# A second level of seven-product multiplication for two of the seven products of Q, gate and up, with column sets chained across pairs

## The chip, the cores and the metric

The kernel runs on one core of one Trainium2 chip. The metric is the device time of one execution in microseconds (us). TensorE is written PE below, its weight loads PEld, VectorE DVE, ScalarE ACT, and SP is the engine that issues the DMAs. Every run reported here is fast, and the granted TensorE clock is 0.998 to 1.000 of full speed in all of them.

A ratio is the mean time of one kernel's fast runs over the mean of the other's fast runs of the same rounds, so it is not quite the ratio of the medians that are quoted beside it. The kernel before takes 747.55 us (median of 4 runs, 746.85 to 748.61).

## The reference

A layer norm feeds two branches. Branch A is linear attention with 32 heads over 2048 tokens, width 1024; branch B is a gated feed-forward layer of width 3584.

```python
xn  = layernorm(x)                                   # 2048 x 1024
q, k, v = split(xn @ wqkv)                           # 1024 x 3072
pq, pk  = phi(q), phi(k)                             # phi(t) = (t > 0 ? t + 1 : exp(t)) + 1e-6
s   = ((pq @ (pk^T v)) / (pq . sum(pk) + 1e-6)) @ wo # per head
b   = (silu(xn @ w_gate) * (xn @ w_up)) @ w_down     # 1024 x 3584, 3584 x 1024
out = x + s * silu(b)
```

## The kernel before

The kernel records every operation with the regions it reads and writes, orders each engine's operations by a list scheduler (earliest deadline first; PE may depart from program order by a window of six groups), and emits fixed instruction streams with semaphore waits. Nearly all operations therefore have one source line, that of a helper: read the groups by what they write and read. `ps` is PSUM (eight banks of 128x512 fp32), `W` holds weights and their sums, `X` and `P` hold the transposed `xn` of the first and second 1024 tokens (the two passes), `H` is the big result area, `TM` holds temporaries.

Already here each matrix product is a block product with seven instead of eight multiplications. One *set* is 256 weight columns against 1024 tokens: the weights are cut into 2 x 2 blocks (halves of K, halves of the columns), so are the tokens, and the seven block products are accumulated in PSUM banks. A product is 4 matmuls (K of 512 in steps of 128) of 512 columns. The sums of weight blocks that products 3, 5, 6 and 7 need are made by DVE when the weights have landed.

```python
def step(self, m):                        # one of the seven products of a set
    if m == 1:
        self.a = balloc(True);  self.grp(1, self.a, True)
        self.b = balloc()
        act(... ps[self.b], ps[self.a], ACT.Identity)        # bank b starts as a copy of P1
    elif m == 5:
        e = balloc(True);       self.grp(5, e, True)
        self.s5 = s5_ring.take();  act(... self.s5, ps[e], ACT.Identity);  bfree(e)
    elif m == 2:                          # P1 + P2 is result (0,0)
        self.grp(2, self.a, False);  self.out(0, 0, self.a)
    elif m == 6:
        self.grp(6, self.b, False);  self.c = balloc()
        tt(... ps[self.c], ps[self.b], self.s5, ALU.add)
    elif m == 7:
        self.grp(7, self.b, False);  d = self.dring.take()
        tt(... d, ps[self.b], self.s5, ALU.add);  self.evac(1, 1, d, ...)
    elif m == 3:  self.grp(3, self.c, False);  self.out(0, 1, self.c)
    elif m == 4:  self.grp(4, self.b, False);  self.out(1, 0, self.b)

# two sets run interleaved as a pair: (set, product)
PAIRSEQ = ((0,1),(0,5),(1,1),(0,2),(1,5),(0,6),(1,2),(1,6),(0,7),(0,3),(1,7),(0,4),(1,3),(1,4))

# --- cut ---
def gu_pair(p, n, stat, at=()):           # a pair is one gate set and one up set
    def ev_g(i, j, ap, r, bank):          # gate: ACT, Silu, PSUM to SBUF
        act(... s.ap(FP16), ap, ACT.Silu)
    def ev_u(i, j, ap, r, bank):          # up: DVE multiplies straight from PSUM into H
        tt(... o, ap, s.ap(FP16), ALU.mult)

order = [("q", 0), ("g", 0), ("q", 1)] + [("g", n) for n in range(1, 14)]   # per pass of 1024 tokens
```

After these 16 pairs a pass has the down products (the D stage, with the attention's last product beside it). The normalisation of the attention (ACT scales a broadcast reciprocal, DVE multiplies) runs beside gate/up pairs 2 and 3.

## Time and profile before

| | before |
|---|---|
| time, median | 747.55 us |
| span of the profiled run | 745.6 us |
| PE busy | 734.1 us (98%), 3522 matmuls |
| DVE busy | 541.1 us (73%) |
| ACT busy | 321.2 us (43%) |

These lines are the first part and the chain of the page: busy time, its share of the span, and the number of instructions; then the chain of work that ended last, by engine.

```profile
span 745.6 us, 9302 instructions
...
PE 734.1 (98%) x3522; PEld 330.4 (44%) x3522; DVE 541.1 (73%) x1010; ACT 321.2 (43%) x532; POOL 16.2 (2%) x35
...
PE 93%; DVE 2%; ACT 2%; DMA 2%; issue 0%; POOL 0%; SPq 0%
...
```

PE is busy almost throughout, and matmuls make 93% of the chain. A busy PE proves little by itself, because the end of a matmul is modelled (379 ns for one of 512 columns, while the next begins after 216). What does prove it is the distance of starts. In the steady gate/up stretch, 56 matmuls take 12.087 us, which is 56 x 215.8 ns. I call *hole* whatever lies between the starts of two neighbouring matmuls beyond what the first takes at its width. The small `Zh` matmuls (the attention's denominators, on 32 columns of the array) are an exception: PE loses about 0.1 us around each group of them with no other engine to wait for, and this is counted with the stream of matmuls, not as holes. Beyond the first 31 us the holes add up to 5.0 us, and 2.2 us of these are the last product's, at the end.

Busy time of each engine by stretches; the first number of a line is the stretch, the second its length. The stretches are Q and the first gate/up sets, the normalisation, steady gate/up with the D stage, the turn of the pass with Q of pass 2, and the normalisation of pass 2.

```profile
...
core 0: us, PE busy (x) PEld busy (x) DVE busy (x) ACT busy (x) POOL busy (x), PEclk, DMA share, GB/s
125.00:200.00 75.00, 74.24 (x358) 31.49 (x356) 55.28 (x109) 40.89 (x72) 0.00 (x0) 1.00 0.48 137
200.00:230.00 30.00, 29.85 (x139) 13.31 (x139) 28.32 (x54) 21.28 (x38) 0.00 (x0) 1.00 0.74 214
230.00:420.00 190.00, 190.00 (x882) 86.00 (x881) 131.56 (x218) 60.66 (x104) 0.00 (x0) 1.00 0.49 124
420.00:480.00 60.00, 59.57 (x286) 24.89 (x285) 44.62 (x86) 31.06 (x47) 0.00 (x0) 1.00 0.38 101
480.00:530.00 50.00, 50.00 (x234) 22.62 (x233) 43.16 (x77) 28.44 (x50) 0.00 (x0) 1.00 0.64 178
...
```

Only the first two and the fourth stretch have any PE idle at all. DVE is the second engine: 131.56 of 190 us in the long stretch.

Groups of instructions (line, engine, operation, written<-read, shapes, number | busy us, mean ns | idle before and what ended it):

```profile
...
L209 PE MATMUL ps<-X,W 128*128 128x512 f16 x1504 | 347.9, 379 | 1.8 <-DVE ps L344 1.2 <-DMA W<-m_scratch 0.5 <-DVE TM L344 0.2
...
L344 DVE TENSOR_TENSOR H<-ps,TM 128x512 f16<-128x512 f32 x84 | 57.3, 689 | 10.8 <-PE ps L209 10.7
...
L337 ACT ACT_TABLE_LOAD x10 | 12.8, 1283 | 1.0 <-PEq L1249 0.8
...
```

The second is up's eviction by DVE. The third: ten loads of an activation table, 1283 ns each, 12.8 us of ACT. They come where Exp (in phi of K and Q) and Silu (gate, D stage) alternate.

### The profile page before, as it was taken

To read this page: it belongs to the slowest core of one execution; us is meant where nothing else is said; L and a number is where in the kernel's file an instruction comes from. 1 tells how busy PE (TensorE), PEld (TensorE's weight loads), DVE (VectorE), ACT (ScalarE), POOL (GpSimd) and SP (SyncE) were. 2 spreads that over 40 slices of the span, in tenths; PEclk is the share of its full clock that TensorE was granted. 3 is DMA by queue.
4 is the path that set the end of the run, shared out by engine and by line. 5 is a ranking of instruction groups with operands and counts; after the bars stand their busy time and mean duration, and the time that the engine had idled before them with its cause. 6 is when DMAs were issued, how large, how long until landed. Compare 5 with 4: busy or idle time off the path is not lost.

```text
span 745.6 us, 9302 instructions
## 1 busy us (share of the span) xinstructions
PE 734.1 (98%) x3522; PEld 330.4 (44%) x3522; DVE 541.1 (73%) x1010; ACT 321.2 (43%) x532; POOL 16.2 (2%) x35
## 2 busy tenths in 40 slices
PE   7999999999999999999999999999999999999997
PEld 3444444434444444444444444344444444444442
DVE  6999757768797776876467677879876768557353
ACT  3677545565574343422232265547533433223131
POOL 2211100000000000000000000000000000000000
PEclk9999999999999999999999999999999999999999
DMA  9353125434682424371846733428627352274822
GB/s 302 94 113 86 29 56 176 108 103 129 191 234 81 113 57 113 100 227 41 199 114 154 181 88 84 114 81 229 203 61 222 104 150 68 68 150 109 193 65 49
DMA packets 168492, 93.92 MB, mean 126 GB/s; under 512 B 33024, under 2 KB 164352, under 8 KB 168448
## 3 DMA queue, kind: packets, MB, share of 16 engines
q1 hardware_dynamic: 168448, 93.34, 47.2%
q8 instruction: 27, 0.44, 0.3%
q14 instruction: 17, 0.14, 0.1%
HBM read 75.50 MB, written 10.62 MB: 115 GB/s over the span
## 4 chain that ended last, share of the span: by engine, by line
PE 93%; DVE 2%; ACT 2%; DMA 2%; issue 0%; POOL 0%; SPq 0%
PE ps L209 93%; DMA W<-m_scratch 1%; ACT H L337 1%; ACT TM L337 1%; DMA W<-in_A_x_dram 0%; DMA H<-r_scratch 0%; DVE TM L344 0%; DVE H L344 0%; ACT L337 0%; PE ps L216 0%; ACT X L337 0%; DVE stats L555 0%; DVE W L344 0%; DVE ps L344 0%; DVE TM L625 0%
## 5 line engine op out<-in xcount | busy, mean ns | idle before, releaser
L209 PE MATMUL ps<-X,W 128*128 128x512 f16 x1504 | 347.9, 379 | 1.8 <-DVE ps L344 1.2
L337 ACT ACTIVATE TM<-ps 128x512 f32<-128x512 f32 (+1 forms) x275 | 162.4, 597 | 252.5 <-PE ps L209 241.5
L209 PEld LDWEIGHTS ps<-X,W 128*128 128x128 f16 (+1 forms) x1504 | 144.6, 98 | 177.6 <-DVE ps L344 3.7
L209 PE MATMUL ps<-H,W 128*128 128x512 f16 (+1 forms) x896 | 205.3, 379 | 0.7 <-DVE TM L625 0.4
L344 DVE TENSOR_TENSOR W<-W 128x1024 f16<-128x1024 bf16 (+3 forms) x224 | 134.2, 628 | 15.4 <-DMA W<-in_B_w_down_dram 6.3
L209 PEld LDWEIGHTS ps<-H,W 128*128 128x128 f16 (+1 forms) x896 | 87.0, 98 | 105.6 <-DVE TM L625 0.9
L209 PE MATMUL ps<-P,W 128*128 128x512 f16 x512 | 123.0, 379 | 0.0
L344 DVE TENSOR_TENSOR ps<-ps,TM 128x512 f32<-128x512 f32 x94 | 65.5, 697 | 71.8 <-PE ps L209 71.7
L337 ACT ACTIVATE ps<-ps 128x512 f32<-128x512 f32 x94 | 55.0, 585 | 98.1 <-PE ps L209 96.1
L344 DVE TENSOR_TENSOR TM<-ps,TM 128x512 f32<-128x512 f32 x88 | 60.2, 684 | 46.3 <-PE ps L209 45.9
L209 PEld LDWEIGHTS ps<-P,W 128*128 128x128 f16 (+1 forms) x512 | 49.3, 98 | 59.3 <-issue 0.2
L344 DVE TENSOR_TENSOR H<-ps,TM 128x512 f16<-128x512 f32 (+1 forms) x91 | 62.1, 688 | 12.1 <-PE ps L209 11.8
L337 ACT ACTIVATE TM<-TM 128x512 f16<-128x512 f32 (+1 forms) x61 | 37.5, 616 | 40.1 <-DVE TM L344 34.9
L344 DVE TENSOR_TENSOR H<-H 128x1024 f16<-128x1024 f16 (+2 forms) x82 | 51.2, 633 | 3.6 <-ACT H L337 2.7
L344 DVE TENSOR_TENSOR TM<-TM 128x512 f16<-128x512 f16 (+1 forms) x63 | 26.0, 421 | 21.5 <-DMA TM<-TM 13.9
L209 PE MATMUL ps<-H,X 128*128 128x512 bf16 (+1 forms) x136 | 32.3, 379 | 1.0 <-ACT X L337 0.7
L624 DVE TENSOR_SCALAR TM<-TM 128x512 f16<-128x512 f16 x64 | 17.7, 288 | 17.3 <-ACT TM L337 16.9
L337 ACT ACTIVATE H<-ps 128x512 bf16<-128x512 f32 (+2 forms) x42 | 24.3, 613 | 11.3 <-PE ps L209 10.9
L344 DVE TENSOR_TENSOR W<-H 128x1024 f16<-128x1024 f16 x38 | 25.7, 686 | 3.7 <-PE ps L209 3.3
L337 ACT ACTIVATE H<-H,zc 128x512 bf16<-128x512 bf16 x32 | 21.6, 715 | 8.6 <-DMA H<-r_scratch 8.6
L209 PE MATMUL ps<-H,P 128*128 128x512 bf16 (+1 forms) x96 | 23.5, 379 | 0.0
L209 PE MATMUL ps<-W 128*128 128x512 f16 x76 | 22.1, 379 | 0.0
(69 smaller groups left out, 287.8 us busy)
## 6 DMA issues: line engine op xcount, KB each, us to landing
W<-in_B_w_gate_dram SPq DMA_DIRECT2D x28, 512.0 KB, 4.1
W<-in_B_w_up_dram SPq DMA_DIRECT2D x28, 512.0 KB, 5.3
W<-in_B_w_down_dram SPq DMA_DIRECT2D x16, 896.0 KB, 6.6
W<-in_A_x_dram SPq DMA_DIRECT2D x16, 256.0 KB, 3.4
H<-in_A_wqkv_dram SPq DMA_DIRECT2D x8, 512.0 KB, 8.1
W<-in_A_wqkv_dram SPq DMA_DIRECT2D x8, 512.0 KB, 5.2
H<-r_scratch SPq DMA_DIRECT2D x32, 128.0 KB, 3.6
q_scratch<-H SPq DMA_DIRECT2D x8, 512.0 KB, 3.9
```

The costliest lines, as they stand in the source:

```text
L209: last = h.matmul(o, l, r, start=st, stop=sp, skip_group_check=True)
L337: return PL.op("act", reads, writes, lambda h: h.activation(o, i, func, **kw), nel(o) / 1200.0 + (0.055 if src == "ps" else 0.095))
L344: return dve(reads, writes, lambda h: h.tensor_tensor(o, a, b, op), nel(o), 1.92 if fast else 0.96)
L624: dve([e.r], [b.r], lambda h: h.tensor_scalar(ba, ea, 1.0, EPS_PHI, ALU.min, ALU.add), 512, 2.6)
```

## The change

The intent is to take columns out of PE's stream. For products 1 and 5, two *neighbouring* sets multiply different weights with the same moving block. Together they are one product of 512 x 256 weights with 512 x 512 tokens, and that is again done in seven instead of eight inner products: K in two halves of 256, columns by set, tokens in two halves of 256. An inner product is two matmuls of 256 columns.

To have neighbouring sets side by side, a pair is now two gate sets or two up sets (512 weight columns, one DMA of 1 MB instead of two of 512 KB). The inner products form a chain of four parts (matmul, ACT copies, matmul, DVE sum, matmul, DVE sum, matmul), so the head of each pair is interleaved with the tail of the pair before, also from the last D set of pass 1 into Q of pass 2. Up is evicted by ACT into H and then multiplied by DVE in 16 bit, and its product 7 goes straight into H. Buffers were moved to make room. The first Q pair of pass 1 has no inner products.

```diff
+        QJ = (((), (1, 5)), ((1, 5), (1, 5)))
+        class Joint:                      # the seven inner products of product 1 or 5 of two sets
+            def step(self, part):
+                if part == 0:
+                    self.x, self.y = balloc(), balloc(True)
+                    self.grp(1, y, 0, True);  self.grp(5, y, 1)          # half banks
+                    act(... ps[x][:, 0:256], ps[y][:, 0:256], ACT.Identity)
+                    self.s = q_ring.take()
+                    act(... self.s, ps[y][:, 256:512], ACT.Identity)
+                elif part == 1:
+                    self.grp(6, y, 0);  self.grp(2, x, 0)
+                    tt(... ps[x][:, 256:512], ps[y][:, 0:256], s, ALU.add)
+                elif part == 2:
+                    self.grp(7, y, 0);  self.grp(3, x, 1)
+                    tt(... ps[y][:, 256:512], ps[y][:, 0:256], s, ALU.add)
+                    self.put(0, x)        # set 0: bank x is its P1 (or P5)
+                elif part == 3:
+                    self.grp(4, y, 0)
+                    self.put(1, y)
-        PAIRSEQ = ((0, 1), (0, 5), (1, 1), ...
+        HEAD = "1_0 5_0 1_1 2_0 5_1 6_0 2_1 6_1".split()
+        TAIL = "7_0 3_0 7_1 4_0 3_1 4_1".split()
+        LINK = "7_0 nj1a 3_0 7_1 nj1b nj5a 3_1 nj1c nj5b 4_0 nj1d nj5c 4_1 n2_0 nj5d n6_0 n2_1 n6_1".split()
 ...
+            for m in joint:               # weight sums of the inner products, in wload
+                sums(A, [tv[:, q] for q in range(4)], [r], tr)
+        def x_inner(v):                   # sums of the moving blocks; B[0,1] is overwritten in place
+            ...
             def ev_u(w): ...
-                tt([r, s.r], [orr], o, ap, s.ap(FP16), ALU.mult)
+                    act([r], [orr], o, ap, ACT.Identity)
+                    tt([orr, s.r], [orr], o, o, s.ap(FP16), ALU.mult, True)
 ...
-        order = [("q", 0), ("g", 0), ("q", 1)] + [("g", n) for n in range(1, NPAIR)]
+        order = [("q", 0), ("g", 0), ("q", 1), ("u", 0)] + [(k, n) for n in range(1, NPAIR // 2) for k in "gu"]
 ... (the last D set of pass 1)
+            if link:
+                seq = "S1 S5 S2 S6 D1 S7 S3 D5 S4 X D6 nj1a D2 nj1b D7 nj1c D3 nj1d nj5a D4 nj5b n2_0 nj5c n6_0 n2_1 nj5d n6_1"
```

More of the change, by code (lines that the diff above doesn't have):

```diff
@@ L406, in build_kernel @@
         s5_ring = Ring(TM, 0, 2 * KB, 2)
-        d_ring = Ring(TM, 4 * KB, 2 * KB, 3)
-        sg_ring = Ring(TM, 10 * KB, 1 * KB, 5)
-        e_ring = Ring(TM, 15 * KB, 1 * KB, 3)
+        d_ring = Ring(TM, 4 * KB, 2 * KB, 2)
+        sg_ring = Ring(TM, 10 * KB, 1 * KB, 10)
+        e_ring = Ring(TM, 20 * KB, 1 * KB, 2)
+        q_ring = Ring(TM, 22 * KB, 1 * KB, 2)
         B_ring = Ring(TM, 24 * KB, 1 * KB, 2)
-        rr_ring = Ring(TM, 18 * KB, 2 * KB, 3)
+        rr_ring = Ring(TM, 20 * KB, 2 * KB, 1)
         fin_ring = Ring(TM, 10 * KB, 1 * KB, 8)
-        xo_ring = Ring(TM, 18 * KB, 2 * KB, 3)
-        pt_ring = Ring(TM, 24 * KB, 1 * KB, 2)
         x_ring = Ring(W, 32 * KB, 2 * KB, 4)
@@ L417, in build_kernel @@
         xs_ring = Ring(W, 16 * KB, 4 * KB, 2)
-        pk_ring = Places([(TM, 18 * KB), (TM, 20 * KB), (TM, 22 * KB), (TM, 10 * KB)], 2 * KB)
+        pk_ring = Ring(TM, 10 * KB, 2 * KB, 4)
         BLK = 4 * 512
@@ L477, in grp, with put1, put5 @@
                     pe_mm(reads, [bank_r[b]], mms)
+            def put1(self, a):
+                self.a = a
+                self.b = balloc()
+                act([bank_r[a]], [bank_r[self.b]], ps[self.b][:, :], ps[a][:, :], ACT.Identity)
+            def put5(self, e):
+                self.s5 = s5_ring.take()
+                act([bank_r[e]], [self.s5.r], self.s5.ap(F32), ps[e][:, :], ACT.Identity)
+                bfree(e)
             def step(self, m):
                 if m == 1:
-                    self.a = balloc(True)
-                    self.grp(1, self.a, True)
-                    self.b = balloc()
-                    act([bank_r[self.a]], [bank_r[self.b]], ps[self.b][:, :], ps[self.a][:, :], ACT.Identity)
+                    a = balloc(True)
+                    self.grp(1, a, True)
+                    self.put1(a)
                 elif m == 5:
@@ L487, in step @@
                     self.grp(5, e, True)
-                    self.s5 = s5_ring.take()
-                    act([bank_r[e]], [self.s5.r], self.s5.ap(F32), ps[e][:, :], ACT.Identity)
-                    bfree(e)
+                    self.put5(e)
                 elif m == 2:
@@ L512, in step, with __init__, grp @@
                     self.out(1, 0, self.b)
-        PAIRSEQ = ((0, 1), (0, 5), (1, 1), (0, 2), (1, 5), (0, 6), (1, 2), (1, 6), (0, 7), (0, 3), (1, 7), (0, 4),
-                   (1, 3), (1, 4))
+        QJ = (((), (1, 5)), ((1, 5), (1, 5)))
+        class Joint:
+            def __init__(self, ops, put):
+                self.ops, self.put = ops, put
+            def grp(self, k, b, h, start=False):
+                pairs, reads = self.ops(k)
+                o = ps[b][:, 256 * h:256 * h + 256]
+                pe_mm(reads, [bank_r[b]], [(o, l, r, start and q == 0, q == len(pairs) - 1)
+                                           for q, (l, r) in enumerate(pairs)])
+            def step(self, part):
+                if part == 0:
+                    self.x, self.y = balloc(), balloc(True)
+                    x, y = self.x, self.y
+                    self.grp(1, y, 0, True)
+                    self.grp(5, y, 1)
+                    act([bank_r[y]], [bank_r[x]], ps[x][:, 0:256], ps[y][:, 0:256], ACT.Identity)
+                    self.s = q_ring.take()
+                    act([bank_r[y]], [self.s.r], self.s.ap(F32), ps[y][:, 256:512], ACT.Identity)
+                    return
+                x, y, s = self.x, self.y, self.s
+                if part == 1:
+                    self.grp(6, y, 0)
+                    self.grp(2, x, 0)
+                    tt([bank_r[y], s.r], [bank_r[x]], ps[x][:, 256:512], ps[y][:, 0:256], s.ap(F32), ALU.add)
+                elif part == 2:
+                    self.grp(7, y, 0)
+                    self.grp(3, x, 1)
+                    tt([bank_r[y], s.r], [bank_r[y]], ps[y][:, 256:512], ps[y][:, 0:256], s.ap(F32), ALU.add)
+                    self.put(0, x)
+                elif part == 3:
+                    self.grp(4, y, 0)
+                    self.put(1, y)
@@ new lines, in build_kernel, with __init__, do @@
+        class Pair:
+            def __init__(self, s0, s1, joint, at):
+                self.sets, self.joint, self.at = (s0, s1), joint, at
+            def do(self, w):
+                if w[0] == "j":
+                    self.joint[w[1]].step("abcd".index(w[2]))
+                else:
+                    self.sets[int(w[2])].step(int(w[0]))
+                    tick()
+                for fn in self.at.get(w, ()):
+                    fn()
+        HEAD = "1_0 5_0 1_1 2_0 5_1 6_0 2_1 6_1".split()
@@ new lines, in build_kernel, with feed @@
+        TAIL = "7_0 3_0 7_1 4_0 3_1 4_1".split()
+        LINK = "7_0 nj1a 3_0 7_1 nj1b nj5a 3_1 nj1c nj5b 4_0 nj1d nj5c 4_1 n2_0 nj5d n6_0 n2_1 n6_1".split()
+        last_pair = [None]
+        def feed(pair):
+            prev = last_pair[0]
+            if pair is None or not pair.joint:
+                if prev is not None:
+                    for w in TAIL:
+                        prev.do(w)
+                if pair is not None:
+                    for w in HEAD:
+                        pair.do(w)
+            else:
+                for w in LINK:
+                    if w[0] == "n":
+                        pair.do(w[1:])
+                    elif prev is not None:
+                        prev.do(w)
+            last_pair[0] = pair
@@ L829, in build_kernel, with sums, wload @@
         raw_ring = Places([(W, o * KB) for o in (0, 8, 16)], 8 * KB)
-        cmb_ring = Places([(W, o * KB) for o in (44, 24, 32)], 8 * KB)
-        def wload(srcs):
+        cmb_ring = Places([(W, o * KB) for o in (24, 32)], 8 * KB)
+        in_ring = Places([(W, o * KB) for o in (44, 46, 40, 42)], 2 * KB)
+        def sums(A, o, rd, wr):
+            tt(rd, [wr[0]], o[0], A[0, 1], A[1, 1], ALU.add, True)
+            tt(rd + [wr[0]], [wr[1]], o[1], o[0], A[0, 0], ALU.subtract, True)
+            tt(rd, [wr[2]], o[2], A[0, 0], A[0, 1], ALU.subtract, True)
+            tt(rd + [wr[1]], [wr[3]], o[3], A[1, 0], o[1], ALU.subtract, True)
+        RAW_OF = {1: (0, 0), 2: (1, 0), 4: (1, 1)}
+        SUM_OF = {5: 0, 6: 1, 7: 2, 3: 3}
+        def wload(src, joint):
             s = raw_ring.take()
-            v = s.ap().rearrange("p (w kt n) -> p w kt n", w=2, n=256)
-            for q, src in enumerate(srcs):
-                dma([], [s.sub(q * 4 * KB, 4 * KB).r], v[:, q], src, dsem("wr%d_%d" % (s.k, q)), 512 * KB)
+            dma([], [s.r], s.ap().rearrange("p (kt n) -> p kt n", n=512), src, dsem("wr%d" % s.k), 1024 * KB)
+            v = s.ap().rearrange("p (kt w n) -> p w kt n", w=2, n=256)
             c = cmb_ring.take()
@@ L840, in wload, with block, jstat @@
             cr = [c.sub(q * 2 * KB, 2 * KB).r for q in range(4)]
-            A = {(k, i): v[:, :, 4 * k:4 * k + 4, i * 128:i * 128 + 128] for k in range(2) for i in range(2)}
-            tt([s.r], [cr[0]], cv[:, 0], A[0, 1], A[1, 1], ALU.add, True)
-            tt([s.r, cr[0]], [cr[1]], cv[:, 1], cv[:, 0], A[0, 0], ALU.subtract, True)
-            tt([s.r], [cr[2]], cv[:, 2], A[0, 0], A[0, 1], ALU.subtract, True)
-            tt([s.r, cr[1]], [cr[3]], cv[:, 3], A[1, 0], cv[:, 1], ALU.subtract, True)
-            def stat(w, m):
-                if m in (1, 2, 4):
-                    k, i = {1: (0, 0), 2: (1, 0), 4: (1, 1)}[m]
-                    return [v[:, w, 4 * k + q, i * 128:i * 128 + 128] for q in range(4)], s.r
-                q4 = {5: 0, 6: 1, 7: 2, 3: 3}[m]
-                return [cv[:, q4, w, q, :] for q in range(4)], cr[q4]
-            return stat
+            sums({(k, i): v[:, :, 4 * k:4 * k + 4, i * 128:i * 128 + 128] for k in range(2) for i in range(2)},
+                 [cv[:, q] for q in range(4)], [s.r], cr)
+            def block(m):
+                if m in RAW_OF:
+                    k, i = RAW_OF[m]
+                    return v[:, :, 4 * k:4 * k + 4, i * 128:i * 128 + 128], s.r
+                return cv[:, SUM_OF[m]], cr[SUM_OF[m]]
+            def stat(w, m):
+                bl, r = block(m)
+                return [bl[:, w, q, :] for q in range(4)], r
+            inner = {}
+            for m in joint:
+                bl, r = block(m)
+                t = in_ring.take()
+                tv = t.ap(FP16).rearrange("p (m kt n) -> p m kt n", m=4, n=128)
+                tr = [t.sub(q * KB // 2, KB // 2).r for q in range(4)]
+                A = {(k, i): bl[:, i, 2 * k:2 * k + 2, :] for k in range(2) for i in range(2)}
+                sums(A, [tv[:, q] for q in range(4)], [r], tr)
+                inner[m] = (A, r, tv, tr)
+            def jstat(m, k):
+                A, r, tv, tr = inner[m]
+                if k in RAW_OF:
+                    return [A[RAW_OF[k]][:, q, :] for q in range(2)], r
+                return [tv[:, SUM_OF[k], q, :] for q in range(2)], tr[SUM_OF[k]]
+            return stat, jstat
         def xset(stat, w, xv, evac, dring):
@@ L860, in xset, with joint_of, ops, f @@
             return Set(ops, evac, dring)
+        IN_AT = (((W, 48 * KB), (W, 49 * KB), (W, 50 * KB)), ((W, 51 * KB), (TM, 8 * KB), (TM, 9 * KB)))
+        xin = {}
+        def x_inner(v):
+            for m, at in zip((1, 5), IN_AT):
+                ap, r = v[XOF[m]]
+                B = {(k, j): ap[:, 2 * k:2 * k + 2, 256 * j:256 * j + 256] for k in range(2) for j in range(2)}
+                t = [(a.at(o, KB, FP16).rearrange("p (k t) -> p k t", t=256), a.reg(o, KB)) for a, o in at]
+                tt([r], [t[1][1]], t[1][0], B[1, 1], B[0, 1], ALU.subtract, True)
+                tt([r], [r], B[0, 1], B[0, 1], B[0, 0], ALU.subtract, True)
+                tt([r], [t[0][1]], t[0][0], B[1, 1], B[0, 1], ALU.subtract, True)
+                tt([r, t[0][1]], [t[2][1]], t[2][0], B[1, 0], t[0][0], ALU.subtract, True)
+                xin[m] = {1: (B[0, 0], r), 2: (B[1, 0], r), 3: (B[1, 1], r), 5: (B[0, 1], r), 6: t[0], 7: t[1], 4: t[2]}
+        def joint_of(jstat, s0, s1):
+            def ops(m):
+                def f(k):
+                    ws, wr = jstat(m, k)
+                    xa, xr = xin[m][k]
+                    return [(ws[q], xa[:, q, :]) for q in range(2)], [wr, xr]
+                return f
+            return {"1": Joint(ops(1), lambda w, b: (s0, s1)[w].put1(b)),
+                    "5": Joint(ops(5), lambda w, b: (s0, s1)[w].put5(b))}
         later = deque()
@@ L875, in flush, with q_load @@
                 later.popleft()[1]()
-        def run_pair(s0, s1, at=()):
-            for n, (w, m) in enumerate(PAIRSEQ):
-                (s0, s1)[w].step(m)
-                tick()
-                for k, fn in at:
-                    if k == n:
-                        fn()
-        def q_load(s):
-            return wload([wqkv_v[:, :, (2 * s + q) * 256:(2 * s + q + 1) * 256] for q in range(2)])
+        def q_load(p, s):
+            return wload(wqkv_v[:, :, s * 512:(s + 1) * 512], QJ[p][s])
         den = {}
@@ L895, in pq_tile, with q_pair @@
             return H.at(o, KB, BF16), H.reg(o, KB)
-        def q_pair(p, s, stat, at=()):
+        def q_pair(p, s, stats, at, go=True):
+            stat, jstat = stats
             def evac(w):
@@ L915, in evac @@
                 return f
-            run_pair(xset(stat, 0, XV[p], evac(0), d_ring), xset(stat, 1, XV[p], evac(1), d_ring), at)
+            s0, s1 = (xset(stat, w, XV[p], evac(w), d_ring) for w in range(2))
+            pair = Pair(s0, s1, joint_of(jstat, s0, s1) if QJ[p][s] else None, at)
+            if go:
+                feed(pair)
+            return pair
         def recip(p):
@@ L972, in hb2, with gu_load @@
             return v, Region(hb(n, nm)[1].keys + hb(n + 1, nm)[1].keys)
-        def gu_load(n):
-            return wload([wg_v[:, :, n * 256:(n + 1) * 256], wu_v[:, :, n * 256:(n + 1) * 256]])
-        def gu_pair(p, n, stat, at=()):
-            sgs = {}
-            def ev_g(i, j, ap, r, bank):
-                s = sg_ring.take()
-                sgs[i, j] = s
-                act([r], [s.r], s.ap(FP16), ap, ACT.Silu, "ps" if bank is not None else "sb")
-            def ev_u(i, j, ap, r, bank):
-                s = sgs[i, j]
-                o, orr = hb(n, "R%d%d" % (i, j))
-                tt([r, s.r], [orr], o, ap, s.ap(FP16), ALU.mult)
-            run_pair(xset(stat, 0, XV[p], ev_g, d_ring), xset(stat, 1, XV[p], ev_u, d_ring), at)
-            if n % 2 == 1:
-                v = {nm: hb2(n - 1, nm) for nm in HOF}
-                tt([v["R11"][1], v["R01"][1]], [v["T3"][1]], v["T3"][0], v["R11"][0], v["R01"][0], ALU.subtract, True)
-                tt([v["R01"][1], v["R00"][1]], [v["T1"][1]], v["T1"][0], v["R01"][0], v["R00"][0], ALU.subtract, True)
-                tt([v["R11"][1], v["T1"][1]], [v["T2"][1]], v["T2"][0], v["R11"][0], v["T1"][0], ALU.subtract, True)
+        def gu_load(k, n):
+            return wload((wg_v if k == "g" else wu_v)[:, :, n * 512:(n + 1) * 512], (1, 5))
@@ new lines, in build_kernel, with gu_pair, ev_g, f @@
+        sgs = {}
+        def gu_pair(p, kind, n, stats, at):
+            stat, jstat = stats
+            def ev_g(w):
+                def f(i, j, ap, r, bank):
+                    s = sg_ring.take()
+                    sgs[w, i, j] = s
+                    act([r], [s.r], s.ap(FP16), ap, ACT.Silu, "ps" if bank is not None else "sb")
+                return f
+            def ev_u(w):
+                def f(i, j, ap, r, bank):
+                    s = sgs[w, i, j]
+                    o, orr = hb(2 * n + w, "R%d%d" % (i, j))
+                    act([r], [orr], o, ap, ACT.Identity)
+                    tt([orr, s.r], [orr], o, o, s.ap(FP16), ALU.mult, True)
+                    if w == 1 and (i, j) == (1, 0):
+                        h_sums(2 * n)
+                return f
+            def direct(w):
+                def f(i, j, b, s5):
+                    s = sgs[w, i, j]
+                    o, orr = hb(2 * n + w, "R%d%d" % (i, j))
+                    tt([bank_r[b], s5.r], [orr], o, ps[b][:, :], s5.ap(F32), ALU.add)
+                    tt([orr, s.r], [orr], o, o, s.ap(FP16), ALU.mult, True)
+                return f
+            s0, s1 = (xset(stat, w, XV[p], (ev_g if kind == "g" else ev_u)(w), d_ring) for w in range(2))
+            if kind == "u":
+                s0.direct, s1.direct = direct(0), direct(1)
+            feed(Pair(s0, s1, joint_of(jstat, s0, s1), at))
@@ L997, in pq_load, with h_sums @@
+        def h_sums(n):
+            v = {nm: hb2(n, nm) for nm in HOF}
+            tt([v["R11"][1], v["R01"][1]], [v["T3"][1]], v["T3"][0], v["R11"][0], v["R01"][0], ALU.subtract, True)
+            tt([v["R01"][1], v["R00"][1]], [v["T1"][1]], v["T1"][0], v["R01"][0], v["R00"][0], ALU.subtract, True)
+            tt([v["R11"][1], v["T1"][1]], [v["T2"][1]], v["T2"][0], v["R11"][0], v["T1"][0], ALU.subtract, True)
         def pq_load(p):
@@ L1006, in build_kernel @@
         GB = 3584
-        t4_ring = Places([(W, 40 * KB), (W, 42 * KB), (TM, 8 * KB)], 2 * KB)
+        rings = ((Ring(TM, 18 * KB, 2 * KB, 3), Ring(TM, 24 * KB, 1 * KB, 2),
+                  Places([(W, 40 * KB), (W, 42 * KB), (TM, 8 * KB)], 2 * KB)),
+                 (Ring(X, 8 * KB, 2 * KB, 3), Ring(X, 14 * KB, 1 * KB, 2),
+                  Places([(W, 40 * KB), (W, 42 * KB)], 2 * KB)))
         dd_ring = Ring(TM, 4 * KB, 2 * KB, 2)
@@ L1062, in d_set @@
             last = (p, c) == (1, 3)
+            link = (p, c) == (0, 3)
+            xo_ring, pt_ring, t4_ring = rings[link]
             def fin(i, j):
@@ L1074, in fin @@
                     dma([], [q.r], xv, xf[row:row + 512, c * 256:(c + 1) * 256].rearrange("(m p) n -> p m n", p=128),
-                        dsem("xo%d" % q.k), 256 * KB).urgent = 60.0 * last
+                        dsem("xo%d%d" % (link, q.k)), 256 * KB).urgent = 60.0 * last
                 q, seen = xo[j]
@@ L1082, in done @@
                         dma([q.r], [], of[row:row + 512, c * 256:(c + 1) * 256].rearrange(
-                            "(m p) n -> p m n", p=128), xv, dsem("oo%d" % q.k), 256 * KB)
+                            "(m p) n -> p m n", p=128), xv, dsem("oo%d%d" % (link, q.k)), 256 * KB)
                 def turn_dma():
@@ L1088, in turn_dma @@
                     PL.op("sp", [g.r], [o.r], lambda h: h.dma_start_transpose(oa, g.ap(FP16)), 0.08,
-                          sem=dsem("tp%d" % o.k), nbytes=200 * KB, urgent=60.0 * last)
+                          sem=dsem("tp%d%d" % (link, o.k)), nbytes=200 * KB, urgent=60.0 * last)
                     tt([o.r, q.r], [q.r], xv[:, :, i * 128:i * 128 + 128], oa, xv[:, :, i * 128:i * 128 + 128], ALU.add,
@@ L1142, in d_set @@
                    "S1 S5 S2 S6 D1 S7 S3 D5 S4 D6 D2 D7 D3 D4")[min(c, 2)]
+            if link:
+                seq = "S1 S5 S2 S6 D1 S7 S3 D5 S4 X D6 nj1a D2 nj1b D7 nj1c D3 nj1d nj5a D4 nj5b n2_0 nj5c n6_0 n2_1 nj5d n6_1"
+                nxt = None
             for w in seq.split():
-                (dset if w[0] == "D" else sset).step(int(w[1]))
-                tick()
+                if w == "X":
+                    nxt = turn_pass()
+                elif w[0] == "n":
+                    nxt.do(w[1:])
+                else:
+                    (dset if w[0] == "D" else sset).step(int(w[1]))
+                    tick()
         tbank = []
         combos(XV[0])
-        order = [("q", 0), ("g", 0), ("q", 1)] + [("g", n) for n in range(1, NPAIR)]
+        order = [("q", 0), ("g", 0), ("q", 1), ("u", 0)] + [(k, n) for n in range(1, NPAIR // 2) for k in "gu"]
         lq = deque([(k, p, n) for p in range(2) for k, n in order])
@@ L1157, in pump @@
             while lq and len(got) < n and lq[0][1] <= gate[0]:
-                k = lq.popleft()
-                got[k] = q_load(k[2]) if k[0] == "q" else gu_load(k[2])
+                k, p, s = lq.popleft()
+                got[k, p, s] = q_load(p, s) if k == "q" else gu_load(k, s)
         pump(2)
@@ L1165, in kv_done, with build_m, turn_pass @@
                 bfree(b)
+        def build_m():
+            if mb:
+                m_build(*mb.popleft())
+        def turn_pass():
+            combos(XV[1])
+            x_inner(XV[1])
+            gate[0] = 1
+            raw_ring.__init__([(W, o * KB) for o in (0, 16, 8)], 8 * KB)
+            cmb_ring.__init__([(X, 0), (W, 24 * KB), (W, 32 * KB)], 8 * KB)
+            in_ring.__init__([(W, o * KB) for o in (44, 46, 40, 42)], 2 * KB)
+            pump(1)
+            last_pair[0] = q_pair(1, 0, got["q", 1, 0], {}, False)
+            return last_pair[0]
         mb = deque((g, c) for g in range(NG) for c in range(2))
@@ L1170, in build_kernel @@
                 st = got.pop((k, p, n))
-                if k == "q":
-                    q_pair(p, n, st, ((4, kv_done), (9, kvt)) if (p, n) == (0, 0) else ())
-                else:
-                    at = ()
-                    if 2 <= n <= 3:
-                        at = tuple((4 + 6 * h, partial(normalise_part, p, n - 2, h)) for h in range(2))
-                    gu_pair(p, n, st, at)
-                pump(2)
-                if p == 0 and n < 2 and k == "g":
-                    for _ in range(8):
-                        if mb:
-                            m_build(*mb.popleft())
-                if (k, n) == ("g", 1):
-                    recip(p)
+                at = {}
+                if (p, k, n) == (0, "q", 0):
+                    at = {"5_1": [kv_done], "3_0": [kvt]}
+                if p == 0 and (k, n) in (("g", 0), ("q", 1), ("u", 0)):
+                    at = {w: [build_m] for w in ("2_1 6_1 7_1 3_1 4_1" + " 2_0" * (k == "u")).split()}
+                if (k, n) == ("u", 0):
+                    at["7_0"] = at.get("7_0", []) + [partial(recip, p)]
+                if n == 1 and k in "gu":
+                    at = {w: [partial(normalise_part, p, "gu".index(k), h)] for h, w in enumerate(("2_1", "7_1"))}
+                if last_pair[0] is not None and (p, k, n) == (1, "q", 0):
+                    pass
+                elif k == "q":
+                    q_pair(p, n, st, at)
+                else:
+                    gu_pair(p, k, n, st, at)
+                if (p, k, n) == (0, "q", 0):
+                    x_inner(XV[0])
+                pump(1)
+            feed(None)
             pq_load(p)
@@ L1189, in build_kernel @@
                 d_set(p, c, Sx, ms)
-            if p == 0:
-                combos(XV[1])
-                gate[0] = 1
-                raw_ring.k = cmb_ring.k = 0
-                pump(2)
         flush()
```

## The prediction

> **What bounds it now.** TensorE. The page gives PE 734.1 of 745.6 us (98%), and the chain that ended last is 93% matmuls. In the timeline, 128x512 matmuls start every 216 ns; after 30 us there are only six holes, some 4 us in all. It shrinks only if fewer columns are streamed. DVE is second: 541 us (73%), 14.1 of 20 us in the steady gate/up stretch 280 to 300 (busy time by stretches).
>
> **What the change removes.** A pair of column sets costs 2 x 7 x 4 = 56 matmuls of 512 columns. Now 40 stay, and products 1 and 5 of both sets become 2 x 7 x 2 = 28 matmuls of 256 columns: 14 wide ones' worth instead of 16. The Trainium skill ("TensorE: Matmul & The Clock Gate", "Wait — 56ns, not 53.3ns?") gives N/2.4 GHz plus 2.5 ns for a warm matmul; the trace agrees at 512 (216 ns) and nearly at 129 columns (59 ns, each with a fresh weight load, so loads stay hidden). So I estimate 109 ns at 256: 56 x 216 = 12.10 us becomes 40 x 216 + 28 x 109 = 11.69 us, 0.4 us per pair. With 3 Q and 28 gate/up pairs: 31 x 0.4 = 12.5 us, all on the critical path.
>
> **What it adds.** DVE occupancy, from back-to-back starts: 128x1024 16-bit 0.60 us, 128x512 16-bit 0.335, 128x512 with PSUM 0.60. The slopes give (estimates) 0.20 us for a 128x256 16-bit sum and 0.34 for a 128x256 PSUM sum, as the Trainium skill has it ("VectorE: DVE Perf Modes", "The perf-mode tier table"): two-tensor operations run double rate on 16-bit SBUF, single rate with PSUM.
> - 248 inner weight sums, 50 us
> - 124 joint PSUM sums, 42 us
> - up: 84 PSUM multiplications (and 28 from SBUF) become ACT evictions and 112 fast ones of 0.335; product 7 goes straight into H. About 30 us less.
>
> Net +65 us. Per gate and up pair together, DVE goes from about 16.6 of 24.2 us to 20.8 of 23.4 us (89%). ACT gets 84 evictions (0.6 us) and 124 half-width copies (about 0.38): +95 us, far from full.
>
> **Is it hidden?** Mostly. Each joint is a chain matmul, ACT copy, matmul, DVE sum, matmul, DVE sum, matmul, with about 1.3 us of other matmuls between links. A link needs about 0.2 us of array drain, 0.42 us for the sum, and up to 0.6 us behind a running DVE operation: 1.2 us. That fits narrowly. For holes where Q's evictions or the normalisation crowd DVE and behind activation-table loads (1.28 us each) I allow 3 us, and 0.7 us back at the joint between the passes.
>
> **Time.** 747.7 - 12.5 + 3 - 0.7 = 737.5 us. Range 733.5 to 745. Faster by over 2%: 4%; within 2%: 90%; slower by over 2%: 6%.
>
> **What would show it.** PE count 3522 to about 3894; 256-wide matmuls at 109 ns; a steady pair in about 11.7 us; DVE busy about 620 us (84%), ACT about 415 us (56%); PE waiting a few us for DVE writes into PSUM; no hole near 435 us.
>
> **What would make it wrong.** DVE misses links regularly: 0.3 us per pair eats 9 us. Or 256-wide matmuls with a weight load each start slower than 109 ns: 13 ns more eats everything. Or the eight PSUM banks, up to seven plus the denominators' in use, make PE wait for evictions in Q.

## The result, and the profile after

The changed kernel takes 739.7 us (median of 4 runs, 739.46 to 740.81) against 747.55; the ratio is 0.9897 with a 95% interval of 0.988 to 0.9914. Run once more as a control on another occasion it took 739.93 us, ratio 0.9902. The results are correct.

The page after, the same lines:

```profile
span 739.1 us, 10502 instructions
...
PE 722.5 (98%) x3878; PEld 365.9 (50%) x3894; DVE 599.3 (81%) x1398; ACT 396.6 (54%) x740; POOL 16.2 (2%) x35
...
PE 86%; ACT 7%; DVE 4%; DMA 1%; issue 1%; SPq 0%; POOL 0%; ACTq 0%
...
```

DVE rose by 58 us and ACT by 75 us. The weight loads (PEld) number 3894, as predicted; 16 of the matmul records are missing from this trace, all of them 512-column bf16 matmuls of four groups (`ps<-H,W`, `ps<-H,X`, `ps<-H,P`, `ps<-H`) in the first 181 us. The chain's share of matmuls fell from 93% to 86%, and ACT's rose from 2% to 7%.

Groups that are new or grew:

```profile
...
L344 DVE TENSOR_TENSOR ps<-ps,TM 128x256 f32<-128x256 f32 x124 | 52.3, 424 | 3.5 <-PE ps L209 3.2
...
L209 PE MATMUL ps<-W 128*128 128x256 f16 x248 | 47.3, 273 | 0.1
L344 DVE TENSOR_TENSOR H<-H,TM 128x512 f16<-128x512 f16 x112 | 45.8, 417 | 12.9 <-ACT H L337 12.5
...
L344 DVE TENSOR_TENSOR W<-W 128x256 f16<-128x256 f16 x131 | 34.5, 281 | 0.0
...
L337 ACT ACTIVATE ps<-ps 128x256 f32<-128x256 f32 x62 | 23.3, 375 | 14.5 <-PE ps L209 13.7 <-DVE ps L344 0.3 <-DVE H L707 0.3
...
L337 ACT ACT_TABLE_LOAD x10 | 12.8, 1283 | 1.0 <-PEq L1430 0.8
...
```

The 273 ns of a 256-column matmul are again a modelled latency; the starts of 667 pairs of neighbours of that width have a median distance of 109 ns. That is the skill's N/2.4 GHz plus 2.5 ns ("TensorE: Matmul & The Clock Gate", "Wait — 56ns, not 53.3ns?"), with a fresh weight load for each. From 245 to 290 us any 68 consecutive matmuls, one pair's worth, take 11.690 us (before: 56 in 12.087 us).

How a chain hides there is seen in the order of time, first on PE, then on DVE. Columns are start, duration, then what, and how many.

```profile
...
284.38 0.38 PE L209 MATMUL ps<-W 128*128 128x256 f16 x2
284.60 1.03 PE L209 MATMUL ps<-X,W 128*128 128x512 f16 x4
285.46 0.38 PE L209 MATMUL ps<-W 128*128 128x256 f16 x2
285.68 0.38 PE L209 MATMUL ps<-TM,W 128*128 128x256 f16 x2
...
```

```profile
...
284.33 0.42 DVE L344 TENSOR_TENSOR ps<-ps,TM 128x256 f32<-128x256 f32 x1
...
284.87 0.42 DVE L344 TENSOR_TENSOR ps<-ps,TM 128x256 f32<-128x256 f32 x1
...
286.41 0.42 DVE L344 TENSOR_TENSOR ps<-ps,TM 128x256 f32<-128x256 f32 x1
...
```

DVE makes one of the two sums at 284.33, the four 512-column matmuls of 284.60 cover it, and the 256-column matmuls that go on with the chains start at 285.46 without any wait shown.

The same stretches as before:

```profile
...
core 0: us, PE busy (x) PEld busy (x) DVE busy (x) ACT busy (x) POOL busy (x), PEclk, DMA share, GB/s
125.00:200.00 75.00, 73.40 (x426) 38.63 (x429) 67.23 (x171) 53.34 (x104) 0.00 (x0) 1.00 0.37 118
200.00:230.00 30.00, 29.15 (x170) 16.08 (x168) 29.14 (x79) 27.32 (x55) 0.00 (x0) 1.00 0.69 205
230.00:420.00 190.00, 190.00 (x982) 95.89 (x981) 148.46 (x324) 81.18 (x160) 0.00 (x0) 1.00 0.45 127
420.00:480.00 60.00, 57.34 (x329) 28.53 (x328) 52.77 (x130) 36.56 (x66) 0.00 (x0) 1.00 0.37 109
480.00:530.00 50.00, 49.88 (x291) 28.07 (x290) 48.66 (x125) 40.83 (x83) 0.00 (x0) 1.00 0.51 160
...
```

In the long steady stretch PE is busy 190.00 of 190 us although DVE rose to 148.46. What was lost was lost elsewhere: the normalisation (29.15 of 30 us) and above all the turn of the pass with Q of pass 2 (57.34 of 60). The largest holes there, on PE, with the time that it idled and who ended it:

```profile
...
439.28 1.03 PE L209 MATMUL ps<-P,X 128*128 128x512 f16 x4
441.23 0.39 PE L209 MATMUL ps<-P,W 128*128 128x256 f16 x2 [0.93 <-DVE H L707]
...
```

```profile
...
447.74 0.40 PE L209 MATMUL ps<-H,Zh 128*32 128x256 bf16 x4
449.17 1.04 PE L209 MATMUL ps<-P,W 128*128 128x512 f16 x4 [1.03 <-ACT ps L337]
```

The second is explained by the same moments on ACT: a table load, then two evictions that queued behind it, then the copy into PSUM for which PE waited.

```profile
...
446.24 1.28 ACT L337 ACT_TABLE_LOAD   x1
447.54 1.08 ACT L337 ACTIVATE TM<-ps 128x512 f16<-128x512 f32 x2
448.51 0.60 ACT L337 ACTIVATE ps<-ps 128x512 f32<-128x512 f32 x1
```

And the waits of PE for its weight loads in all (engine, line, waited for whom: us in total, times, longest):

```profile
...
PEld ps L209 <- DVE ps L344: 3.5, 11, 0.5
PEld ps L209 <- ACT ps L337: 3.3, 5, 1.3
...
PEld ps L209 <- DVE H L707: 2.5, 4, 1.4
...
PEld ps L209 <- ACT TM L337: 2.2, 7, 0.8
...
```

Before, the first of these groups was:

```profile
...
PEld ps L209 <- DVE ps L344: 4.0, 9, 1.3
...
```

Neither of the two ACT groups reached 0.3 us then. So the new chains did not make PE wait longer for DVE's sums; they made it wait for ACT, and for DVE's evictions of Q (L707 into H).

The sum for the two profiled runs, with holes taken from the starts of matmuls in the traces (where the 16 records are missing, the time that those matmuls take is not counted as a hole; the control and the runs e9 to e11 lack 16 records too):

| us | before | after |
|---|---|---|
| matmuls at their widths, with the switches at `Zh` (stream) | 729.8 | 716.9 |
| holes in the first 31 us | 5.5 | 6.3 (control 5.5) |
| holes after 31 us | 5.0 | about 10.1 |
| of these: 31 to 125 (K, V) | 0.2 | 1.1 |
| 125 to 200 (Q, first sets) | 1.2 | 1.6 |
| 200 to 230 (normalisation) | 0.0 | 1.3 |
| 230 to 420 (steady, D stage) | 0.1 | 0.1 |
| 420 to 480 (turn of pass, Q) | 0.6 | 3.5 |
| 480 to 530 (normalisation) | 0.0 | 0.4 |
| 530 to the end | 2.9 | 2.2 |
| last matmul to the end of the span | 3.6 | 4.2 |

The stream became 12.9 us shorter (12.3 us by the widths alone, 725.9 to 713.6 us) and the holes 5.1 us longer. The 0.5 us more after the last matmul was not pursued.

### The profile page after: what moved, and what is told of

Its sections match the earlier page's. It is cut to its first block, busy times and chain, and to the rows that moved or that the text cites. A ratio compares the mean times of both kernels' runs of the same rounds, so it can differ in the third digit from the quotient of the medians.

```text
span 739.1 us, 10502 instructions
## 1 busy us (share of the span) xinstructions
PE 722.5 (98%) x3878; PEld 365.9 (50%) x3894; DVE 599.3 (81%) x1398; ACT 396.6 (54%) x740; POOL 16.2 (2%) x35
## 4 chain that ended last, share of the span: by engine, by line
PE 86%; ACT 7%; DVE 4%; DMA 1%; issue 1%; SPq 0%; POOL 0%; ACTq 0%
PE ps L209 86%; ACT TM L337 3%; ACT H L337 3%; DMA W<-in_A_x_dram 1%; ACT L337 1%; DVE H L707 1%; DVE W L344 1%; ACT ps L337 1%; DVE TM L706 0%; ACT W L337 0%; DVE H L344 0%; PE ps L216 0%; DVE TM L344 0%; DVE stats L637 0%; ACT X L337 0%
## 5 line engine op out<-in xcount | busy, mean ns | idle before, releaser
L209 PE MATMUL ps<-X,W 128*128 128x512 f16 (+1 forms) x1408 | 312.9, 361 | 1.1 <-ACT ps L337 0.9
L337 ACT ACTIVATE TM<-ps 128x512 f16<-128x512 f32 (+2 forms) x337 | 182.0, 557 | 156.6 <-PE ps L209 154.0
L344 DVE TENSOR_TENSOR W<-W 128x256 f16<-128x256 f16 (+6 forms) x424 | 170.0, 440 | 7.8 <-DMA W<-in_B_w_down_dram 5.7
L344 DVE TENSOR_TENSOR ps<-ps,TM 128x256 f32<-128x256 f32 (+1 forms) x218 | 117.5, 540 | 34.1 <-PE ps L209 33.1
L337 ACT ACTIVATE H<-ps 128x512 f16<-128x512 f32 (+1 forms) x126 | 75.3, 602 | 64.6 <-PE ps L209 64.4
L337 ACT ACTIVATE ps<-ps 128x512 f32<-128x512 f32 (+1 forms) x156 | 78.7, 505 | 57.6 <-PE ps L209 52.6
L209 PE MATMUL ps<-P,W 128*128 128x256 f16 (+1 forms) x440 | 90.0, 323 | 2.1 <-ACT ps L337 1.0
L209 PE MATMUL ps<-W 128*128 128x256 f16 (+1 forms) x328 | 70.3, 299 | 0.5 <-DVE W L344 0.3
L344 DVE TENSOR_TENSOR TM<-ps,TM 128x512 f32<-128x512 f32 (+1 forms) x60 | 40.9, 682 | 31.2 <-PE ps L209 30.9
L344 DVE TENSOR_TENSOR H<-H,TM 128x512 f16<-128x512 f16 x112 | 45.8, 417 | 12.9 <-ACT H L337 12.5
```

The lines of the kernel that those rows point to most:

```text
L209: last = h.matmul(o, l, r, start=st, stop=sp, skip_group_check=True)
L337: return PL.op("act", reads, writes, lambda h: h.activation(o, i, func, **kw), nel(o) / 1200.0 + (0.055 if src == "ps" else 0.095))
L344: return dve(reads, writes, lambda h: h.tensor_tensor(o, a, b, op), nel(o), 1.92 if fast else 0.96)
```

## The experiments

Theory 1: the gain is the arithmetic, 0.4 us per pair, and the chains hide because of what stands between their links. Theory 2: DVE, by estimate at 89% of a gate and up pair, is near its limit and makes the new holes. Theory 3: ACT makes them. Each edit is against the changed kernel.

| run | edit | us, median | ratio to before (95%) | holes after 31 us |
|---|---|---|---|---|
| changed kernel | | 739.70 | 0.9897 (0.988 to 0.9914) | 10.1 |
| e12_after_again | none (control) | 739.93 | 0.9902 (0.9887 to 0.9917) | 10.1 |
| e1_no_inner | no inner products, 30 of 31 pairs | 747.22 | 0.9988 (0.9973 to 1.0003) | 4.7 |
| e2_unchained | chains not interleaved | 778.14 | 1.0404 (1.0389 to 1.042) | 47.7 |
| e3_up_on_dve | up evicted by DVE | 739.53 | 0.9886 (0.987 to 0.9903) | 9.7 |
| e7_inner_twice | inner sums made twice | 742.37 | 0.9925 (0.991 to 0.994) | 12.6 |
| e4_no_q_inner | two Q pairs without inner products | 739.57 | 0.989 (0.9875 to 0.9905) | 8.0 |
| e5_scale_on_dve | normalisation scaled by DVE | 739.63 | 0.9895 (0.988 to 0.9909) | 9.4 |
| e6_q_first | both Q pairs first | 738.20 | 0.9879 (0.9862 to 0.9897) | 7.7 |
| e8_no_tables | Identity for Silu | 736.16 | 0.985 (0.9834 to 0.9867) | 6.4 |
| e9_qfirst_up | e6 and e3 | 737.37 | 0.9869 (0.9855 to 0.9884) | 7.5 |
| e10_qfirst_swap | e6, D4 before D3 in the link | 738.18 | 0.9881 (0.9865 to 0.9898) | 8.0 |
| e11_all_three | e6, e3 and the swap | 737.11 | 0.9864 (0.985 to 0.9879) | 7.4 |

### Is it the arithmetic? e1_no_inner

```diff
-QJ = (((), (1, 5)), ((1, 5), (1, 5)))
+QJ = (((), ()), ((1, 5), ()))
-    wload((wg_v if k == "g" else wu_v)[...], (1, 5))
+    wload((wg_v if k == "g" else wu_v)[...], ())
-    feed(Pair(s0, s1, joint_of(jstat, s0, s1), at))
+    feed(Pair(s0, s1, None, at))
```

> The seven inner products are taken out of 30 of the 31 pairs (the one between the passes keeps them), all else of the change stays. Theory 1 (the gain is the arithmetic: 0.4 us of matmul columns per pair, all on the critical path): 12 us of columns come back, some holes of the Q and normalising stretches go, so 747 to 751 us, ratio to before 1.000 to 1.004. Rival (the gain is from the rest: up evicted by ACT, whole-row weight loads of 1 MB, the linked pass): 737 to 743 us.

Measured: 747.22 us, ratio 0.9988; the time before is back. The result is wrong: the sums of the moving blocks are still made, and they overwrite a quarter of the blocks that the plain products 1 and 5 read. The instructions and waits are those of a plain kernel, so the time stands. Its stream is 729.5 us and its holes 4.7 us, both like before. The other parts of the change (larger weight loads, up by ACT, the linked pass) are worth nothing measurable alone. Theory 1 holds.

### What hides the chains? e2_unchained

```diff
-    for w in LINK: ...
+    for w in TAIL: prev.do(w)
+    for w in "j1a j5a j1b j5b j1c j5c j1d j5d 2_0 6_0 2_1 6_1".split():
+        pair.do(w)
```

> The inner products stay, but are not interleaved with the tail of the pair before: only the two inner chains alternate with each other. Theory 1 (the chain links are hidden only because about 1.3 us of other matmuls stand between them): each of three links then has 0.44 us of cover for 0.8 to 1.2 us of latency, some 0.5 us of hole per link, 1 to 1.5 us per pair, 31 pairs: 765 to 790 us. Rival (the scheduler's window of six groups, which may pull tail products forward, covers it anyhow): 739 to 745 us.

Measured: 778.14 us, correct. That is 38.4 us over the changed kernel, 1.2 us for each of the 31 pairs, within what was expected. The scheduler's window does not replace the order. One steady chain on PE:

```profile
...
248.71 0.39 PE L209 MATMUL ps<-X,W 128*128 128x256 f16 x2 [0.24 <-ACT ps L337]
249.00 0.39 PE L209 MATMUL ps<-W 128*128 128x256 f16 x2
249.28 0.39 PE L209 MATMUL ps<-X,W 128*128 128x256 f16 x2
249.57 0.74 PE L209 MATMUL ps<-W 128*128 128x256 f16 x4
...
```

Two inner matmuls take 0.22 us, but the next two start only after 0.28 or 0.29 us, and ahead of 248.71 PE idled until ACT's copy was there. On DVE, the first of the four sums in these moments:

```profile
...
249.43 1.93 DVE L344 TENSOR_TENSOR ps<-ps,TM 128x256 f32<-128x256 f32 x4 [1.97 <-PE ps L209]
...
```

DVE had idled 1.97 us, waiting for PE: the engine that was thought crowded had nothing to do. Latency, not load, makes these holes.

### Is DVE at its limit? e3_up_on_dve and e7_inner_twice

```diff
 # e3_up_on_dve
-    act([r], [orr], o, ap, ACT.Identity)
-    tt([orr, s.r], [orr], o, o, s.ap(FP16), ALU.mult, True)
+    tt([r, s.r], [orr], o, ap, s.ap(FP16), ALU.mult)
-    if kind == "u":
-        s0.direct, s1.direct = direct(0), direct(1)
 # e7_inner_twice
     sums(A, [tv[:, q] for q in range(4)], [r], tr)
+    sums(A, [tv[:, q] for q in range(4)], [r], tr)
```

> Up's eviction goes back to DVE, multiplying from PSUM. DVE occupancy up by about 30 us, to about 98% of a gate and up pair (estimate). Theory 2 (DVE's load is near its limit, and the eviction by ACT was needed): holes in gate/up, 742 to 749 us. Rival (DVE still has room, the eviction by ACT was not needed): 739 to 741 us.

> Each inner weight sum is made twice: 248 more DVE operations of 128x256, +50 us of DVE occupancy, to about 103% of a gate and up pair by my estimate. Theory 2 (DVE within about a tenth of its limit): DVE bounds gate/up, 747 to 760 us. Rival (DVE at 81% has ample room): 739 to 742 us.

Measured: e3_up_on_dve 739.53 us, as fast as the changed kernel, so here theory 2 missed and its rival was right. e7_inner_twice 742.37 us, between the two expectations: 42 us more of DVE's busy time cost 2.7 us. Busy time of e3_up_on_dve in steady gate/up, and in the stretch around it:

```profile
...
240.00:300.00 60.00, 60.00 (x349) 33.96 (x347) 60.00 (x139) 26.86 (x58) 0.00 (x0) 1.00 0.28 92
300.00:340.00 40.00, 40.00 (x200) 19.45 (x199) 34.46 (x59) 11.82 (x23) 0.00 (x0) 1.00 0.51 152
340.00:400.00 60.00, 60.00 (x279) 27.10 (x278) 34.12 (x69) 17.16 (x29) 0.00 (x0) 1.00 0.59 148
...
```

DVE is busy 60.00 of 60 us and PE does not miss anything. The scheduler puts the earliest deadline first, so the sums that PE waits for precede multiplications, sums of H and weight sums of later pairs. The backlog is worked off before 340 us (34.46 of 40 us busy; the changed kernel has 31.34), and then DVE is as idle as in the changed kernel (34.12 of 60 us, against 33.78). So here a secondary engine at 100% over 60 us was no limit: its urgent work went first, and a stage with room followed. That the buffers would have filled had the stage come later is my reading, not shown. With e7_inner_twice the room ends: its steady stretch of pass 1 shows no holes either, but in the second 1.0 us of PE is missing, with DVE busy 80.00 of 80 us:

```profile
...
560.00:640.00 80.00, 78.99 (x428) 40.66 (x426) 80.00 (x206) 41.82 (x85) 0.00 (x0) 1.00 0.42 130
...
```

So the limit is real, but, roughly, it lies above the changed kernel's load by more than the 24 us of busy time that e3_up_on_dve added and less than the 42 us of e7_inner_twice (622.9 and 641.0 against 599.3 us). Evicting up by ACT was not needed for the time.

### Do Q's inner products make the holes? e4_no_q_inner

```diff
-QJ = (((), (1, 5)), ((1, 5), (1, 5)))
+QJ = (((), ()), ((1, 5), ()))
```

> Two of the three Q pairs (the second of each pass) lose their inner products; the first of pass 2 keeps them, being the link. 0.8 us of columns come back. Their result is wrong, since one set of moving operands is overwritten for the inner products; the instructions and waits are as they would be. Theory 3a (the new holes in the Q stretches come from the inner chains' extra work there): 2 us of holes go, 738 to 739 us. Rival (the holes near Q come from activation-table loads and the denominators whatever the products are): 740 to 741 us.

Measured: 739.57 us (738.66 to 739.76). Its output is wrong, which doesn't matter for the time. The holes of its trace fell by 2 us and the stream grew by 0.9, but the times do not differ from the changed kernel's or the control's clearly. Inconclusive: whether Q should have inner products is open within about 1 us either way.

### Do the normalisation's scalings on ACT make them? e5_scale_on_dve

```diff
-act([z_r, zrr], [zrr], zr, zr, ACT.Identity, "sb", scale=zc[:, g:g + 1])
+dve([z_r, zrr], [zrr], lambda h, zr=zr, g=g: h.tensor_scalar(zr, zr, zc[:, g:g + 1], None, ALU.mult), 512, 3.84)
```

> The 32 scalings of the normalisation go from ACT (0.61 us each back to back) to DVE as tensor_scalar operations, 0.20 us each. Theory 3b (the holes at 210, 223 and 515 us, 1.6 us together, are joint copies that wait behind these scalings on ACT): they go, 737.5 to 738.5 us. Rival (it is DVE that is crowded there, at 97 to 99%): no change or worse, 739.5 to 741 us.

Measured: 739.63 us, no change; the rival's number. In the changed kernel the cause at 210 us is plain to see on ACT, five scalings and then the copy for which PE waited:

```profile
...
207.70 3.19 ACT L337 ACTIVATE H<-H,zc 128x512 bf16<-128x512 bf16 x5
210.76 0.40 ACT L337 ACTIVATE ps<-ps 128x256 f32<-128x256 f32 x1
...
```

With the scalings on DVE the hole at 210 us shrank from 0.58 to 0.07 us, so that reading was right for it. But at 223 us 0.49 of 0.74 us stayed, now ended by a DVE sum, and 0.24 us appeared at 528 us. The wait went from one engine to the other. The normalisation's 1.7 us of holes became 1.1, too little to show in the time.

### Do table loads make them? e8_no_tables and e6_q_first

```diff
 # e8_no_tables (wrong on purpose)
-ap, ACT.Silu, ...          # gate, and the D stage
+ap, ACT.Identity, ...
 # e6_q_first
-order = [("q", 0), ("g", 0), ("q", 1), ("u", 0)] + ...
+order = [("q", 0), ("q", 1), ("g", 0), ("u", 0)] + ...
```

> Every Silu is replaced by Identity, on purpose wrong, so that one activation table serves the kernel: table loads fall from 10 to 1, no other instruction changes. Theory 3c (the table loads, 1.28 us each, make the holes at 138, 155 to 163 and 437 to 448 us): 735 to 737 us. Rival (they are made by DVE's evictions of Q and by the PSUM banks): 738.5 to 740 us.

> Both Q pairs stand before the first gate pair: activation-table loads fall from 10 to 6, 5 us less of ACT. Theory 3c (table loads in front of the joint copies and evictions make the Q holes): 736.5 to 738.5 us. Rival (two Q pairs in a row crowd DVE, which needs more than 14 us for each in 13 us of matmuls, and PSUM banks come free late): 740 to 745 us.

Measured: e8_no_tables 736.16 us, e6_q_first 738.20 us and correct; both within the expectation of the table-load theory. No other instruction of e8_no_tables differs: nine loads of 1.28 us, 11.5 us of an engine that is busy 54% of the time, cost 3.5 us of the whole. The turn of the pass and Q:

```profile
...
125.00:200.00 75.00, 74.89 (x441) 39.69 (x439) 68.65 (x176) 51.24 (x104) 0.00 (x0) 1.00 0.40 122
...
420.00:480.00 60.00, 59.52 (x347) 30.38 (x345) 54.70 (x141) 32.33 (x67) 0.00 (x0) 1.00 0.33 97
...
```

PE is busy 59.52 of 60 us there instead of 57.34, and 74.89 of 75 in Q of pass 1 instead of 73.40, no worse than in the kernel before (59.57 and 74.24). The holes from 420 to 480 us fell from 3.5 to 1.1 us. That includes the one that PE's view laid at a DVE eviction of Q (1.09 us at 440 us, 0.18 us without the loads): DVE's eviction needs ACT's Exp, and the Exps were late. The engine that ends a wait is not always the one that caused it. The normalisation's holes stay, 1.3 us at 200 to 230 us, as they should if those are a separate cause.

The holes can now be accounted for. Of the changed kernel's 10.1 us, 3.7 go with the table loads (6.4 us are left in e8_no_tables), and 1.7 are the normalisation's of both passes. What remains, 4.7 us, is about the 5.0 us of the kernel before.

The Trainium skill says to do all functions of one table set before switching ("ScalarE: Activation LUTs", "Table sets: the hidden batching unit"). With both Q pairs first there are 6 loads instead of 10, and 1.5 us are gained by the medians (the intervals of the two ratios overlap a little; the holes fell from 10.1 to 7.7 us).

### Do the causes add? e9_qfirst_up, e10_qfirst_swap, e11_all_three, with e12_after_again as control

```diff
 # e10_qfirst_swap: e6_q_first, and
-nj1c D3 nj1d nj5a D4 nj5b n2_0 ...
+nj1c D4 nj1d nj5a D3 nj5b n2_0 ...
 # e9_qfirst_up: e6_q_first with e3_up_on_dve.  e11_all_three: all of these
```

> The changed kernel once more, unaltered, as a control beside the three below on the same chip: 739.5 to 740 us, ratio 0.989 to 0.990.

> Q first (6 table loads) and up's eviction back on DVE together. If the holes near 208 and 220 us are joint copies behind a crowded ACT, taking 84 evictions off ACT shortens them as it did alone (1.3 us to 0.3 us), on top of the 1.5 us of Q first: 736.8 to 737.8 us. Rival (DVE, at 100% for long stretches, has no more room with two Q pairs in a row): 738 us or more.

> Q first, and in the link between the passes the last two down products change places, so that all their Silu evictions come before Q's first Exp: 4 table loads in place of 6. Table-load theory: the holes at 434 to 438 us (1.5 us) shrink, 736.8 to 737.8 us. Rival (that hole is DVE's eviction of Q, held by nothing on ACT): 738 to 738.5 us.

> Q first, the swap in the link, and up's eviction on DVE. If the causes are separate their gains add: 735.5 to 737 us, the best of all, about 1.5% under before. If they share one cause: 737 to 738 us.

Measured: control 739.93, e9_qfirst_up 737.37, e10_qfirst_swap 738.18, e11_all_three 737.11 us.

e9_qfirst_up meets its expectation, and of the two holes at 208 and 220 us (1.3 us) 0.3 us are left. In e3_up_on_dve, where up's eviction is the only edit, the normalisation's first holes fell from 1.3 to 0.3 us as well. That says that in the normalisation the crowd on ACT was the cause, as up's 84 evictions were a part of it.

e10_qfirst_swap did what was asked of ACT (4 loads) and the holes at 434 to 438 us fell from 1.5 to 0.4 us, but the time is e6_q_first's: product D4 comes earlier, its operands are sums that DVE makes just before, and 1.0 us of new holes at 421 to 424 us wait for those; a hole at 459 us grew by 0.2. Its theory was right for the hole and the repair paid for it elsewhere.

e11_all_three at 737.11 us misses its expectation of adding gains by a little and falls into the other one: Q first and up on DVE give nearly all of it, and the swap adds nothing clear. It is the best correct version: ratio 0.9864 to before, and its interval (0.985 to 0.9879) lies wholly below the control's (0.9887 to 0.9917) on the same chip, though not below e9_qfirst_up's.

## Why the prediction was right or wrong

The forecast was 737.5 us, range 733.5 to 745, within 2% at 90%. The measured 739.7 us is in the range and within 2%; of the predicted gain of about 10 us, 7.9 came.

- **What bounds it: right.** PE's column stream is the time. A version without the inner products is back at 747.22 us.
- **What is saved: right.** Predicted 12.5 us, 0.4 us per pair; measured 12.9 us of stream (12.3 by widths alone), 12.087 to 11.690 us per pair, 109 ns per 256-column matmul.
- **What is added: nearly right.** DVE 599 us against 620, ACT 397 against 415 predicted. For ACT the estimate took each operation's whole duration (0.6 and 0.38 us), while back to back they start every 0.49 and 0.28 us. For DVE the occupancies were right (0.20 and 0.33 us measured), and its own sum, 541 + 65, is 606.
- **The chains hide: right, by the margin named.** No holes in steady gate/up; without the interleaving 1.2 us per pair are lost.
- **The step that failed is the hole term**: "For holes where Q's evictions or the normalisation crowd DVE and behind activation-table loads (1.28 us each) I allow 3 us, and 0.7 us back at the joint between the passes." That is 2.3 us net; it measured 5.1 us (5.0 to about 10.1). The 0.7 us did not come back: the stretch round the joint went from 0.6 to 3.5 us of holes, and "no hole near 435 us" was wrong, as the worst lie there. The table loads, which I had named last, cost 3.5 us by e8_no_tables. Before the change the same ten loads cost less: all holes of the two Q stretches came to 1.8 us then, 0.9 us of it at 154 us and 0.5 us at 438 us, each soon after a load. How much of this the loads made, and whether it is the chain of short links through ACT that makes them dearer now, is not shown, since the kernel before was not run without table loads.
- **DVE as the danger: wrong.** I watched the engine with the highest share. DVE took 24 us more of busy time at no cost, and the new waits are for ACT, at 54% of the span. "PE waiting a few us for DVE writes into PSUM" is 3.5 us after and 4.0 us before.
- **PSUM banks** were not tested by a run of their own; that they make some of the remaining Q holes stays open.

## What to carry to other kernels

When PE is the limit, count the columns taken out: that part of a forecast was right within 4%. For the rest, look not at which engine has the highest share but at which has long operations in front of a link that cannot be put behind it: an engine with deferrable work can run at 100% for 60 us for nothing, while an engine at 54% with 1.28 us table loads in its queue cost 3.5 us here, with short chains passing through it. Order the functions of ACT by table set before adding such chains, and when an engine ends a wait, look at what that engine itself had been waiting for.

## What the Trainium skill lacked or had wrong

- "TensorE: Matmul & The Clock Gate", "Back-to-back issue gap": it gives about 131 ns per matmul at N=512 and about 81 ns at N=128 for a sustained stream of weight loads and matmuls. These runs show 216 ns at 512, 109 ns at 256 and 59 ns at 129 columns, each with a fresh weight load; the formula that the page calls the isolated one is what held (216, 109 and 56 ns).
- "TensorE: Matmul & The Clock Gate", Part 3, "The mechanism": its list of what overlaps says that weight loads overlap matmuls in flight only where the row groups differ; the paragraph above that list also allows a load into the background weight buffer. Here every matmul uses all 128 rows, its weight load takes 98 ns in the trace, and 256-column matmuls still start every 109 ns, so the list's "only" does not hold here.
- "ScalarE: Activation LUTs", "What ACT_TABLE_LOAD costs": it gives 1283 ns for the load and about 1380 ns of drain with it, about 2.66 us for every switch. The traces show the 1283 ns but not the drain: where evictions are queued, as at 432.56 us after the change, the load starts 19 ns after the end of the activation before it, and the next activation starts 11 ns after the load.
- No page says how a load of tables on an engine with much idle time acts on another engine that waits for it: nine loads, 11.5 us, were worth 3.5 us here.
